# A long-convolution block and a token MLP on one core: the shift filter as diagonal matrices on TensorE, and spectra with real and imaginary parts on the partition halves

## The chip, the cores and the metric

The kernel runs on one core of a Trainium2 chip. The metric is the device time of one execution in microseconds (us). The kernel before was timed in three runs; where one number stands for it, it is their median.

## The reference, cut to what matters

All activations are bf16, S = 2048 rows by D = 448 channels.

```
q' = layernorm(x)                                 # x = A_q
k_shift[t] = sum over j=0..3 of k[t-j] * shift_k[:, j]     # causal, 4 taps per channel
kv = k_shift * v
y  = irfft(rfft(pad(kv)) * rfft(pad(ssm_k)))[:S]  # per channel, length 2S
y  = y + kv * ssm_D
h  = x + q' * y
u  = gelu(layernorm(layernorm(h)) mixed over tokens with w1 (2048x1792) + b1)
out = h + (u mixed with w2 (1792x2048) + b2)
```

So there are two parts: a convolution along the sequence by a spectrum product, and an MLP that mixes tokens. The parameter A_ssm_D is added into the filter at its first tap.

## The kernel before, in words

**Layout.** A row t of the sequence is q*16 + r, with q on the 128 partitions and r = 0..15 as a free dimension. All data lie in one SBUF tensor called arena, cut by byte offsets, so every instruction of the profile shows arena and ps (PSUM, eight banks of 448 f32 used).

**Fourier transform in two stages.** Stage 1 (emit_stage1) multiplies each r by two 128x128 tables E (cosine and sine over q), 2 matmuls of 448 columns, L933. It is done for the filter ssm_k (tag k, 16 values of r) and for kv (tag u, 16). A PSUM pair of 896 f32 is evacuated by ScalarE alone (L943) into one of eight ring buffers, and DMA transfers scatter it over partitions (L947): one of 112 rows from the POOL queue, and one of 16 rows from SP's. When all r of a tag have landed, stage 2 (emit_stage2, L964) combines them with the table FW. Its matmuls are tiled by columns: FW's left half makes real parts and its right half imaginary parts, each for 64 partitions, and two j share the partitions (par). So the real and imaginary part of a frequency lie on the same partition. The results go back over their inputs TK (filter) and TU (u), by evac, on ScalarE or VectorE (L652 to L656).

**The filter's transposes.** emit_kT transposes ssm_k, loaded as KN, on TensorE (L914) into eight PSUM banks, each for two values of r; a bank is complete when all four channel blocks have come.

**The shift filter (emit_kv).** k is loaded with a halo of three rows as KH (19 rows per partition). The four tap rows are spread to all partitions by four matmuls with a row of ones (L868). For each r VectorE multiplies four shifted rows by the taps, 1792 elements (L879); TensorE adds the four by matmuls with the identity (L885); VectorE multiplies the sum from PSUM by v, in place in V (L888). V is stage 1's input for u.

**Spectrum product and first inverse stage (emit_products_i1).** VectorE forms all four products of real and imaginary parts, 1792 elements (L1015). Matmuls tiled by rows, 64 partitions each (L1027), combine them with the tables MA, MN and MB. The results are evacuated to TU and scattered to TZ by DMA (L1051; the last pair of j in smaller transfers per half of channels, L1040, from three queues). emit_ct makes the transposed tables ET for the last stage. Before the last stage TensorE runs 34 filler matmuls (emit_warm, L1061) while the transfers land.

**Last stage and MLP.** emit_i2 (L1118) makes y for each r, then gate, residual and norms give Q. emit_mlp runs 112 + 112 matmuls with the halves W1A and W1B of w1 (L1218, L1228) and gelu (L1208), and 224 with w2 (L1238), with the residual by VectorE (L1242). w1 and w2 are loaded by SP (emit_w1_load, emit_w2_load): the first half of W1A after the last POOL transfer of u's stage 1, the rest after the last POOL transfer of i1.

**What sets the order.** All operations are recorded first, with what they read and write. A list scheduler then runs a model with estimated durations and writes a fixed order for every engine. Priorities are due times, the constants T_..., smaller first: T_K1 and T_DK1 for the filter's stage 1, T_U1 for u's, T_U2 and T_K2 for the two stage 2, T_I1 for products, T_KV for the shift filter. Operations recorded with FX = ("act", "dve") may go to either engine. In hardware each engine keeps that order and waits on semaphores. SP's queue carries all loads and the small shuffle transfers; POOL carries the large shuffle transfers and small arithmetic.

Of the kernel before, what the change touches and what calls it, by code (L numbers as in the profile page):

```python
# [509 lines left out]
def _build(nc, A_q, A_k, A_v, A_shift_k, A_ssm_k, A_ssm_D, B_w1, B_b1, B_w2, B_b2, out):  # L510
# [8 lines left out]
    R = 16  # L519
# [18 lines left out]
    o_W1A = 0  # L538
# [4 lines left out]
    o_W1B = o_V  # L543
    o_E = o_V + 14336
    o_WT = o_E + 8192
    o_SK = o_WT + 3584
# [14 lines left out]
    o_SM = o_BD + 4 * 256  # L561
# [4 lines left out]
    with ctx:  # L566
# [20 lines left out]
        KH = view(o_KH, [R + 3, D])  # L587
# [4 lines left out]
        TK = view(o_TK, [R, 2, D])  # L592
        W1B = view(o_W1B, [R, 896])
# [8 lines left out]
        WT = view(o_WT, [4, D])  # L602
        SK = view(o_SK, [4 * D])
# [4 lines left out]
        FW, MA, MB, MN = [view(o_BD + 256 * k, [128], f16) for k in range(4)]  # L608
# [30 lines left out]
        T_KV, T_DKV, T_KT, T_K1, T_DK1, T_U1, T_DU1 = -37.75, 0.96, -26.42, -39.56, 0.44, 2.72, 0.9  # L639
        T_K2, T_U2, T_D2, T_CT, T_BIAS, T_I1, T_DI1 = 29.29, -14.6, 1.375, 22.37, 56.3, 7.01, 0.974  # L640
        T_Q, T_DQ, T_I2, T_DI2, T_M1, T_W1 = 83.98, 14.35, 85.76, 0.401, 102.98, 122.45

        T_TH, T_TN = -36.0, -30.0
# [17 lines left out]
        def emit_tables():  # L661
# [125 lines left out]
            for k, (dst, i) in enumerate(((FW, 0), (MA, 1), (MB, 1))):  # L787
# [3 lines left out]
            op("pool", lambda e, W: e.tensor_scalar(out=MN, in0=MA, scalar1=-1.0, scalar2=None, op0=ALU.mult),  # L791
               r=[(o_BD + 256, 256)], w=[(o_BD + 768, 256)], n=128)
# [6 lines left out]
        r_iv = [(o_BD + 256, 768)]  # L799
# [4 lines left out]
        def emit_loads():  # L804
            Dq = "sp"
            for i, c in enumerate((3, 0, 1, 2)):
# [4 lines left out]
            op(Dq, lambda e, W: e.dma_start(SK[0:1, :], A_shift_k.rearrange("(a d) j -> a (d j)", a=1)),  # L811
               w=[(o_SK, 3584)], dmab=3584, keng=1)
            op("pool", lambda e, W: e.memset(KH[0:1, 0:3, :], 0.0), w=[(o_KH, 3 * DB, "halo")], n=3 * D)
            for c in range(4):
                sch.t0 = -14.0 + c
                op(Dq, lambda e, W, c=c: e.dma_start(KH[:, 3 + 4 * c:7 + 4 * c, :], k2d[:, 4 * c:4 * c + 4, :]),
                   w=[(o_KH + (3 + 4 * c) * DB, 4 * DB)], dmab=128 * 4 * DB)
                if c == 3:
                    sch.t0 = -10.5
                    op(Dq, lambda e, W: e.dma_start(KH[1:113, 0:3, :], k2d[0:112, 13:16, :]),  # L820
# [14 lines left out]
        def emit_xload():  # L835
            for c in range(4):
                sch.t0 = T_XL + c
                op("sp", lambda e, W, c=c: e.dma_start(X[:, 4 * c:4 * c + 4, :], x2d[:, 4 * c:4 * c + 4, :]),
                   w=[(o_X + 4 * c * DB, 4 * DB)], dmab=128 * 4 * DB,
                   after=[shuf["upool15"]])  # L840

        o_b1n = small(256)
        o_b2n = small(32)
        o_b2c = small(64)
        o_b1c = small(64)
# [452 lines left out]
```

## Time and profile before

| what | us |
|---|---|
| median of three runs | 191.09 (188.78, 191.09, 193.0) |
| span of the profiled execution, first to last instruction | 186.8 |
| busy PE / DVE / ACT / POOL | 173.8 / 109.9 / 97.3 / 72.0 |
| first stage-1 evacuation (L943) starts | 15.6 |
| first L964 (filter stage 2) starts | 39.7 |
| last product with v (L888) starts | 46.5 |
| last stage-1 transfer issued from POOL | 50.4 |
| last L1015 ends | 80.0 |
| i2 (L1118) starts | 87.8 |
| last L1242 ends | 184.6 |

The page does not give a time of the profiled execution beside its span; the median of the runs is 4.3 us above the span. In the profile PE is TensorE's matmuls, PEld its weight loads, DVE VectorE, ACT ScalarE, POOL GpSimd, SP the engine that issues most transfers. A group's row gives line, engine, operation, output and input, count, busy time, mean duration of one, and idle time ahead of it with what ended it. Matmuls overlap, so 352 ns for one is not its cost: 224 of them take 42.39 us in the chain of work that ended last. Most of evac's work stands under L652 and L653 (ScalarE) and L655 and L656 (VectorE), whichever stage it serves.

### The profile page before, as it was taken

What the parts mean: (1) busy time and instruction counts of PE and PEld (TensorE: products, weight loads), DVE (VectorE), ACT (ScalarE), POOL (GpSimd) and SP (SyncE); (2) the same over time, 40 slices, a digit from 0 to 9 for tenths busy, and PEclk for the clock granted to TensorE, in tenths of its full rate; (3) what the DMA queues carried; (4) which work ended last, traced back from release to release, by engine and by line L of the source; (5) the groups of instructions that cost most, each with busy time, mean ns of one, the idle gap of its engine ahead of it and who ended that gap; (6) DMA issues with size and microseconds to landing.
All of it is one profiled execution on the core that took longest, in us unless ns stands there. A gap on an engine that the chain in (4) does not pass through costs nothing.

```text
span 186.8 us, 2835 instructions
## 1 busy us (share of the span) xinstructions
PE 173.8 (93%) x1033; PEld 91.8 (49%) x1033; DVE 109.9 (59%) x181; ACT 97.3 (52%) x141; POOL 72.0 (39%) x177
## 2 busy tenths in 40 slices
PE   7998897998988989899989999999999999999993
PEld 2753342343332433244435445555557777777772
DVE  8877999787789999997979756000001122212221
ACT  3597989988889989950886483442121000000000
POOL 8946976699520044587178676000000000000000
DMA  5998698888549916773999999900000100111111
GB/s 140 419 418 303 179 244 219 228 226 250 141 111 383 365 49 194 220 233 102 329 400 401 423 421 422 364 4 0 0 0 4 49 32 17 49 53 49 49 49 49
DMA packets 15893, 35.44 MB, mean 190 GB/s; under 512 B 3901, under 2 KB 10062, under 8 KB 15878
## 3 DMA queue, kind: packets, MB, share of 16 engines
q1 hardware_dynamic: 11222, 25.66, 36.5%
q0 software_dynamic: 4608, 9.56, 18.3%
q8 instruction: 8, 0.13, 0.3%
q14 instruction: 7, 0.06, 0.1%
q10 hardware_dynamic: 48, 0.03, 0.0%
HBM read 22.37 MB, written 1.84 MB: 130 GB/s over the span
## 4 chain that ended last, share of the span: by engine, by line
PE 72%; DMA 9%; ACT 7%; DVE 6%; POOL 2%; issue 2%; SPq 0%; ACTq 0%
PE ps L1238 23%; PE ps L1228 11%; PE ps L1218 10%; DMA arena<-arena 7%; PE ps L1061 5%; PE ps L1027 5%; ACT arena L652 4%; PE ps L964 4%; PE ps L1118 3%; PE ps L914 2%; DMA arena<-in_A_ssm_k_dram 2%; PE ps L885 2%; DVE arena L1015 2%; POOL arena L947 2%; PE ps L933 2%
## 5 line engine op out<-in xcount | busy, mean ns | idle before, releaser
L1242 DVE SCALAR_TENSOR_TENSOR arena<-ps,arena 128x448 bf16<-128x448 f32 x16 | 10.9, 683 | 56.9 <-PE ps L1238 56.9
L1238 PE MATMUL ps<-arena 128*128 128x448 bf16 x224 | 42.5, 352 | 0.0
L1238 PEld LDWEIGHTS ps<-arena 128*128 128x128 bf16 x224 | 32.3, 144 | 10.1
L943 ACT CAST arena<-ps 128x896 bf16<-128x896 f32 x32 | 26.8, 927 | 3.6 <-PE ps L933 1.7
L652 ACT CAST arena<-ps 128x896 bf16<-128x896 f32 (+1 forms) x26 | 22.0, 908 | 2.6 <-PE ps L868 1.7
L1218 PE MATMUL ps<-arena 128*128 128x448 bf16 x112 | 23.0, 353 | 0.3 <-DVE arena L1173 0.2
L947 POOL DMA_DIRECT2D arena<-arena x32 | 19.2, 601 | 7.6 <-ACT arena L943 4.9
L1228 PE MATMUL ps<-arena 128*128 128x448 bf16 x112 | 21.4, 352 | 0.0
L1208 ACT ACTIVATE arena<-ps,arena 128x448 bf16<-128x448 f32 x14 | 8.2, 640 | 20.1 <-PE ps L1228 14.7
L879 DVE TENSOR_TENSOR arena<-arena 128x1792 bf16<-128x1792 bf16 x16 | 18.2, 1175 | 0.0
L964 PE MATMUL ps<-arena 128*64 128x448 bf16 x128 | 16.4, 361 | 1.8 <-ACT arena L652 1.0
L1125 ACT ACTIVATE arena<-ps,arena 128x448 f32<-128x448 f32 x16 | 11.2, 723 | 12.2 <-PE ps L1118 9.2
L933 PE MATMUL ps<-arena 128*128 128x448 bf16 x64 | 16.1, 355 | 1.3 <-ACT arena L943 1.3
L885 PE MATMUL ps<-arena 128*128 128x448 bf16 x64 | 14.5, 353 | 2.4 <-ACT arena L943 1.8
L1015 DVE TENSOR_TENSOR arena<-arena 128x1792 bf16<-128x1792 bf16 x16 | 16.4, 1083 | 0.0
L1218 PEld LDWEIGHTS ps<-arena 128*128 128x128 bf16 x112 | 10.9, 98 | 11.1 <-DVE arena L1173 1.1
L1051 POOL DMA_DIRECT2D arena<-arena x14 | 8.2, 588 | 20.8 <-PE ps L964 15.6
L1228 PEld LDWEIGHTS ps<-arena 128*128 128x128 bf16 x112 | 11.0, 98 | 10.2
L1027 PE MATMUL ps<-arena 64*128 64x448 bf16 x128 | 14.1, 351 | 1.3 <-DVE arena L1015 0.6
L1132 DVE SCALAR_TENSOR_TENSOR arena<-arena 128x448 f32<-128x448 bf16 x16 | 10.7, 676 | 4.7 <-ACT arena L1125 4.7
L655 DVE CAST arena<-ps 128x896 bf16<-128x896 f32 (+2 forms) x11 | 9.5, 875 | 2.7 <-PE ps L868 1.2
L964 PEld LDWEIGHTS ps<-arena 128*64 128x64 f16 x128 | 5.4, 108 | 11.4 <-ACT arena L652 4.6
(88 smaller groups left out, 200.7 us busy)
## 6 DMA issues: line engine op xcount, KB each, us to landing
arena<-arena POOLq DMA_DIRECT2D x46, 196.0 KB, 5.1
arena<-in_B_w_dram SPq DMA_DIRECT2D x8, 896.0 KB, 9.2
arena<-in_B_w_dram SPq DMA_DIRECT2D x2, 2048.0 KB, 17.2
arena<-in_B_w_dram SPq DMA_DIRECT2D x2, 1536.0 KB, 19.9
arena<-in_A_k_dram SPq DMA_DIRECT2D x4, 448.0 KB, 7.5
arena<-in_A_v_dram SPq DMA_DIRECT2D x4, 448.0 KB, 8.1
arena<-in_A_q_dram SPq DMA_DIRECT2D x4, 448.0 KB, 4.9
out_dram<-arena SPq DMA_DIRECT2D x7, 224.0 KB, 1.9
```

The costliest lines, as they stand in the source:

```text
L652: return e.copy(out=dst(), in_=src())
L879: op("dve", lambda e, W, T=T, i=i, r=r: e.tensor_tensor(out=T[:, i], in0=KH[:, r:r + 4, :], in1=WT, op=ALU.mult), r=[(o_KH + r * DB, 4 * D ...
L885: op("pe", lambda e, W, b=b, T=T, i=i, j=j: e.matmul(Pb(b, i), ID, T[:, i, j, :], start=(j == 0), stop=(j == 3)), r=[(o_ID, 256), (o + (i ...
L933: op("pe", lambda e, W, b=b, r=r, h=h, dl=dl: e.matmul(Pb(b, h), E[:, 2 * r + h, :], src[:, r, :], start=True, stop=not dl), r=[r_E(r), (o ...
L943: return e.copy(out=dst, in_=Ppair(b)) if W == "act" else e.tensor_copy(out=dst, in_=Ppair(b))
L947: shuf[tag + q_ + str(r)] = shuf[tag + q_] = op(q_, lambda e, W, w=w, p0=p0, a=a, b_=b_, j0=j0: e.dma_start(T[p0:p0 + 29:4, j0:j0 + (b_ - ...
L964: op("pe", lambda e, W, b=bs[h], h=h, j=j, c=c, par=par: e.matmul(PS[64 * par:64 * par + 64, b.slots[c], 0:D], FW[:, 64 * c:64 * c + 64], ...
L1015: op("dve", lambda e, W, m=m, i=i: e.tensor_tensor(out=MR(m.slots[0]).rearrange("p (x y) d -> p x y d", x=2), in0=TU[:, i].unsqueeze(2).br ...
L1027: k = op("pe", lambda e, W, b=bs[h], m=ms[h], par=par, t=t, tab=tab, xy=xy, P=P: e.matmul(Pb(b, par), tab[P, :], MR(m.slots[0])[P, xy, :], ...
L1218: op("pe", lambda e, W, r=r, fc=fc, b=bs[fc]: e.matmul(Pb(b), W1A[:, r, 128 * fc:128 * fc + 128], Q[:, r, :], start=(r == 0), stop=(r == R ...
L1228: op("pe", lambda e, W, r=r, fc=fc, b=b: e.matmul(Pb(b), W1B[:, r, 128 * (fc - n0):128 * (fc - n0) + 128], Q[:, r, :], start=(r == 0), sto ...
L1238: op("pe", lambda e, W, r=r, fc=fc, b=b: e.matmul(Pb(b), W2[fc // 7][:, fc % 7, r:S:R], G[:, fc, :], start=(fc == 0), stop=(fc == NFC - 1) ...
```

## The change

Three things are changed together, and due times with them.

1. **Shift filter.** k is loaded without halo. It is transposed on TensorE, 64 transposes of 128 rows by 112 channels, and evacuated to KX with channels on the partitions; a column of zeros stands where row −1 would be. A table DG holds for each block of 112 channels four diagonal matrices of taps. Matmuls of KX against DG, seven for each group of four r and block of channels, add all taps of all shifts in PSUM, with rows on the partitions again. VectorE multiplies by v as before.
2. **Spectra.** Stage 2 uses FW whole: one PSUM pair for each j, real parts on partitions 0–63 and imaginary parts on 64–127. The product needs the filter also with the halves exchanged: KS, filled from TK by eight transfers on SP's queue, two for each four j (N_SW). One product of 1792 elements makes both sums' terms, and four full matmuls for each j replace the tiled ones. Half of MA changes sign, and MN falls away.
3. **Others.** Stage 1's evacuation may go to either engine. The filter's transposes are evacuated by blocks of eight r and one channel block. The last transfers of i1 are like the others. W1A and W1B change places in the arena, since KS lies at its beginning.

The diff, cut to its core:

```diff
-    o_W1A = 0
+    o_KS = 0
+    o_W1B = 0
...
-    o_W1B = o_V
+    o_W1A = o_V
...
-        T_KV, T_DKV, T_KT, T_K1, T_DK1, T_U1, T_DU1 = -37.75, 0.96, -26.42, -39.56, 0.44, 2.72, 0.9
-        T_K2, T_U2, T_D2, T_CT, T_BIAS, T_I1, T_DI1 = 29.29, -14.6, 1.375, 22.37, 56.3, 7.01, 0.974
-        T_Q, T_DQ, T_I2, T_DI2, T_M1, T_W1 = 83.98, 14.35, 85.76, 0.401, 102.98, 122.45
-        T_TH, T_TN = -36.0, -30.0
+        T_KV, T_DKV, T_KT, T_K1, T_DK1, T_U1, T_DU1 = -35.67, 2.8, -45.99, -40.62, 0.9, -24, 0.433
+        T_K2, T_U2, T_D2, T_CT, T_BIAS, T_I1, T_DI1 = 45.17, -14.6, 1.375, 8.48, 50.16, 8.91, 1.558
+        T_Q, T_DQ, T_I2, T_DI2, T_M1, T_W1 = 80.1, 14.35, 82.13, 0.501, 102.98, 122.45
+        T_TH, T_TN = -45.27, -29.29
+        N_SW = 4
+        T_KX = -39.65
...
-            op("pool", lambda e, W: e.tensor_scalar(out=MN, in0=MA, scalar1=-1.0, scalar2=None, op0=ALU.mult),
+            op("dve", lambda e, W: e.tensor_scalar(out=MA[64:128], in0=MA[64:128], scalar1=-1.0, scalar2=None, op0=ALU.mult),
...
+            op("dve", lambda e, W: e.tensor_tensor(
+                out=DG[0:112].rearrange("p c j d -> p (c j) d"), in0=ID[0:112, 0:112].unsqueeze(1).broadcast_to([112, 16, 112]),
+                in1=wsc[0:112].unsqueeze(2).broadcast_to([112, 16, 112]), op=ALU.mult),
+               r=[(o_ID, 256), (o_wsc, 64)], w=[(o_DG, 3584)], n=1792, kind="1x")
+            for g in (3, 0, 1, 2):
+                for cc in range(2):
...
+                            op("pe", lambda e, W, b=b, i=i, rr=rr, r=r, c=c: e.transpose(
+                                out=Pbf(b, 0)[0:112, 512 * i + 128 * rr:512 * i + 128 * rr + 128],
+                                in_=KH[:, r, 112 * c:112 * c + 112], identity=ID),
...
+            for g in range(4):
+                for cc in range(2):
...
+                        for dl in (0, -3, -2, -1, 1, 2, 3):
...
+                            op("pe", lambda e, W, b=b, i=i, cc=cc, dl=dl, i0=i0, i1=i1, rs=rs, sh=sh: e.matmul(
+                                Pb(b, i)[:, 112 * i0:112 * i1 + 112], KX[cc][0:112, i, rs, sh:sh + 128],
+                                DG[0:112, 2 * cc + i, i0 - dl:i1 - dl + 1, :].rearrange("p j d -> p (j d)"),
+                                start=(dl == 0), stop=(dl == 3)),
...
-                op("act", fn, br=[b], bw=[w], n=2 * D, kind="psum")
+                op(FX, fn, br=[b], bw=[w], n=2 * D, kind="psum")
...
+            for j in range(R):
+                sch.t0 = (T_K2 if scale else T_U2) + T_D2 * j
+                b = _Buf(psum, 2)
                 for h in range(2):
+                    op("pe", lambda e, W, b=b, h=h, j=j: e.matmul(Pb(b, h), FW, T[:, j, h, :], start=True, stop=True),
+                       r=r_fw + [(o_T + (2 * j + h) * DB, DB)], bw=[b], n=D)
+                evac(lambda j=j: T[:, j], lambda b=b: Ppair(b), [(o_T + j * 2 * DB, 2 * DB)], b, 2 * D, scale=scale)
+                if scale and j % N_SW == N_SW - 1:
+                    j0 = j + 1 - N_SW
+                    for h in range(2):
+                        op("sp", lambda e, W, j0=j0, h=h: e.dma_start(
+                            KS[64 * h:64 * h + 64, j0:j0 + N_SW].rearrange("p j c d -> p (j c d)"),
+                            TK[64 - 64 * h:128 - 64 * h, j0:j0 + N_SW].rearrange("p j c d -> p (j c d)")),
...
+                op("dve", lambda e, W, m=m, j=j: e.tensor_tensor(
+                    out=MR(m.slots[0]).rearrange("p (x h) d -> p x (h d)", x=2),
+                    in0=TU[:, j].rearrange("p h d -> p (h d)").unsqueeze(1).broadcast_to([128, 2, 2 * D]),
+                    in1=KK[:, :, j * 2 * D:(j + 1) * 2 * D], op=ALU.mult),
...
+                for x, tab in enumerate((MB, MA)):
                     for h in range(2):
+                        k = op("pe", lambda e, W, b=b, m=m, h=h, x=x, tab=tab: e.matmul(
+                            Pb(b, h), tab, MR(m.slots[0])[:, 2 * x + h, :], start=(x == 0), stop=(x == 1)),
+                           r=r_iv, br=[m], bw=[b], n=D)
```

## The prediction

> **What bounds the kernel now.** I read the page first (busy shares, the forty slices), then the chain that ended last in order of time, then the busy time of each engine by stretch, then the groups with shapes kept apart. The page's forty slices part the span into a front and an MLP:
>
> ```profile
> PE   7998897998988989899989999999999999999993
> DVE  8877999787789999997979756000001122212221
> ACT  3597989988889989950886483442121000000000
> DMA  5998698888549916773999999900000100111111
> ```
>
> From slice 20 on TensorE is full and the rest is nearly idle. That part is 448 matmuls at 0.19 us (chain: L1218, L1228 and L1238; 42.39 us for 224 of them), and the change does not touch it. So only the start of i2, the inverse stage, counts. It stands at 87.78 us and the end follows 99.0 us later. I cut the front at the marks that the timeline gives: first stage-1 evacuation (15.6), first stage-2 result of u (54.0), last i1 evacuation (82.0), first i2 matmul (87.8). The columns are length, then busy us (instructions) of PE, PEld, DVE, ACT, POOL, granted clock, DMA share, GB/s:
>
> ```profile
> 15.60:54.00 38.40, 33.84 (x192) 13.77 (x190) 32.93 (x36) 34.72 (x43) 29.18 (x56) 1.00 0.74 210
> 54.00:82.00 28.00, 25.27 (x221) 9.64 (x222) 26.46 (x31) 26.32 (x31) 8.72 (x15) 1.00 0.71 231
> 82.00:87.80 5.80, 5.73 (x32) 2.79 (x30) 5.35 (x17) 0.00 (x0) 5.55 (x13) 1.00 0.52 160
> ```
>
> In both long stretches VectorE and ScalarE are the fullest (DVE 86% and 94%, ACT 90% and 94%). PE's busy time counts overlapping 352 ns matmuls; at the chain's 0.19 us each its work in the first stretch is about 30 us of 38.4. The third stretch is one latency: the last results' way through the DMA, covered on PE by 34 fillers of L1061. The chain shows how u reaches its end:
>
> ```profile
> 41.55 0.77 PE ps L885 x4
> 42.31 0.02 issue
> 42.34 1.09 DVE arena L888
> 43.43 2.01 DVE arena L879
> 45.44 0.04 issue
> 45.48 0.93 PE ps L885 x4
> ...
> 47.85 0.50 PE ps L933 x2
> 48.35 0.02 issue
> 48.38 0.92 ACT arena L943
> ```
>
> The shift filter's products (L879) stand on VectorE ahead of the last u matmuls (L933). The groups concerned, with count, busy us, mean ns, idle before:
>
> ```profile
> L879 DVE TENSOR_TENSOR arena<-arena 128x1792 bf16<-128x1792 bf16 x16 | 18.2, 1175 | 0.0
> L943 ACT CAST arena<-ps 128x896 bf16<-128x896 f32 x32 | 26.8, 927 | 3.6 <-PE ps L933 1.7 <-PE ps L937 1.4 <-DMA arena<-arena 0.4
> L888 DVE TENSOR_TENSOR arena<-ps,arena 128x896 bf16<-128x896 f32 x8 | 8.7, 1090 | 3.1 <-PE ps L885 3.0
> L1015 DVE TENSOR_TENSOR arena<-arena 128x1792 bf16<-128x1792 bf16 x16 | 16.4, 1083 | 0.0
> L655 DVE COPY arena<-ps 128x1024 f16<-128x1024 f16 x1 | 0.7, 678 | 0.0
> L652 ACT COPY arena<-ps 128x1024 f16<-128x1024 f16 x3 | 3.0, 1012 | 1.4 <-PE ps L996 1.4
> ```
>
> L879 never waits: VectorE is always late there.
>
> [...] L879 and L1015 take 1.08 to 1.18 us for 1792 elements, L888 1.09 us for 896. [...] 448 KB loads land after 4.9 us (q) and 7.5 us (k). [...] No 64-partition transfer is in the trace before.
>
> **The change, part by part.**
>
> *Removed from VectorE:* 16 L879, 18.2 us, one of them before 15.6; so 17 us from the first stretch. Four tap-row evacuations (L655 three at 0.62, L652 one at 0.53) leave the time before 15.6. *Added:* eight evacuations of transposed k, 1024 elements bf16 from PSUM: 1.01 us on ACT, 0.68 on DVE (the last two rows above), 0.85 as a mean, 6.8 us. One product that makes the diagonals, 1792 elements with an f32 factor: L751 has 1024 elements of 32 bits in 1.21 us, so 1.2 to 2.1 us; I take 2.0, half of it before 15.6. The sign flip of half a table moves from POOL (0.58) to DVE, between 0.15 us (L742, one element) and 0.28 (L783, 128 elements); 0.2. The eight L888 and all other evacuations keep number and size; those of transposed ssm_k become six of 1024 and two of 512 in place of eight of 896, the same sum. Net on the two engines from 15.6: −17 + 6.8 + 1.0 + 0.2 = −9.0 us. L943 may now also go to DVE, so the saving can be shared. The two engines carry 120.4 us in the 66.4 us from 15.6 to 82.0, a density of 0.907 each. At equal density, (120.4 − 9.0)/(2 × 0.907) = 61.4 us: **−5.0 us**. If the saving stays on DVE while ACT's 61.0 us remain, it is near 0; if the density rises too, −7. I keep −5.0.
>
> *TensorE.* Off: four L868 at 0.48 us, 1.9 us, all in the chain. The filter's 64 matmuls of 448 columns become 112 with the same 28,672 columns; at 0.19 us per 448 that is 12.1 us[...]; I take 13, +0.9. 64 transposes at 0.062 us (chain: 0.74 us for 12 L914): +4.0. Stage 2: 128 tiled matmuls at 0.124 (0.99 us for 8) become 64 at 0.19, −3.7 in two stages. i1: 128 at 0.105 (4.20 us for 40) become 64 at 0.19, −1.2. Sum about −1.9 us, but +3 in the first stretch, where PE has about 8 us left; it is hidden behind the evacuations, else costs those 3.
>
> *The start.* Without the 1.9 us of L868 and without the halo loads (294 and 39 KB, landing 10.8 us after issue), but with the diagonals ahead of u and fresh PSUM evacuations per half: between −2 and +1; **−1.2 us**.
>
> *The exchanged copy.* Eight SP issues of 458,752 B each, 3.67 MB. A pair of halves: [...]7.5 us by the k-load row. Each waits for four evacuations of the filter's stage 2, and behind it in SP's order stand the small parts of u's shuffles, whose landing u2 awaits, then the x and w1 loads. The product L1015 gains a wait: behind it on DVE are evacuations, and i1's matmuls wait for it. In bytes it takes 8.7 us of all DMA engines at 420 GB/s (the load slices), 13 at 282 (210 GB/s over a share of 0.74). The DMA has 26% of 38.4 = 10 us free in stretch one and 8 in stretch two. So it fits mostly in the gaps; it gives nothing back, since it only adds bytes and a wait, and at most it is the 4.8 to 7.4 us of rival (b). I take **+1.2 us**.
>
> *The tail.* The last pair's transfers are no longer cut in half-width pieces: they land after the normal median 5.1 us, not 4.5: **+0.6**, between 0 and 1.5. The two or three issues it saves on POOL and ACT are hidden by L1061.
>
> *Moved at no cost:* both halves of w1 change place. The first is loaded over V, last read at 49.1 and loaded at 55.7; the second over the copy, last read at 80.0 and loaded at 89.1. Covered by these gaps; uncovered, a w1 quarter costs its 9.2 us landing. POOL loses a 1.2 us memset and a table and gains small ones; its 32 shuffle issues every 0.81 us (0.59 and a 0.22 gap) need 26 us of stretch one, so POOL is next in line when that stretch falls under about 30. ACT's finer share needs no waits beyond PSUM.
>
> **Sum:** −5.0 − 1.2 + 1.2 + 0.6 = −4.4 us. The profile's span is 186.8; the profiled execution's whole time is not given, and the runs' median lies 4.3 us above the span, which I take as what lies around it: 191.1. With −4.4 it is **186.7 us**.
>
> **The rivals.**
> (a) *The DMA, or PE, takes over stretch one.* 28.4 us of DMA there (0.74 × 38.4) plus 8.7 to 13 for the copy is 37 to 41 us: if all of the copy falls before u2, u's shuffles end no sooner, and only the gain on stretch two is left. For it: 0.78 share already in 30 to 50 us. Against it: slices 10 and 11 are at 5 and 4 tenths. Time 190.0.
> (b) *The copy of the last filter group comes late: slower.* In the profile the last four filter evacuations (L653) run from 68.7 to 76.1, after u2, since filter stage 2 has the lowest priority; it keeps it. If so again, landing adds 4.9 to 7.5 us (81 to 83.6); then four products at 1.03, four matmuls and an evacuation (5.8 us): 86.8 to 89.4 in place of 82.0. With little gained ahead of it: 196 to 198.5, say 197. It decides if that group is evacuated after about 70 us. Against it: VectorE, relieved, has room before u2.
> (c) *More is freed than summed.* All of filter stage 2 goes before u2, so stretch two holds 32 evacuations and 16 products: 22.4 us at full density against 28, and stretch one still shrinks by three: 182.
> That the work does not leave VectorE is excluded: L879 is gone from the code.
>
> **Numbers.** Forecast 0.43 (range of its own 183 to 189.5), (a) 0.19, (b) 0.30, (c) 0.08. A difference of 2%, about what a measurement of this kernel can tell from no change, is 187.3 below and 194.9 above. Of the forecast's 0.43, 0.30 lie below 187.3; with (c), faster 0.38. Same: 0.13 + 0.19 = 0.32. Slower 0.30. The range 183 to 197 leaves out about half of (c) and half of (b), 0.19.
>
> **What would show it.** Right: no DVE group of sixteen 1.1 us products ahead of u; casts of stage 1 on both engines; u2 starting at 50 to 52 and i2 at about 83.4; MLP still 99.0 us long. The start: first stage-1 evacuation by 14.5. Wrong by (a): u2 at 54 or later with a DMA share above 0.9 in stretch one. Wrong by (b): DVE or PE idle before L1015's successor, ended by a DMA arena<-arena, and the filter's last evacuation after 70. Wrong by the tail: more than 6.5 us from the last i1 evacuation to i2.

## The result, and the profile after

The changed kernel took 202.51 us (median of four runs, 200.81 to 205.7), the kernel before beside it 190.7. The ratio is **1.068, interval 1.057 to 1.080**: slower by 6.8%, where 186.7 us and faster were forecast. Executions of one kernel differ (31 of the kernel before took 188.05 to 193.23 us), so ratios, here and below, compare only those within about 1.5% of a kernel's fastest; the medians of all runs give 1.062 here. The profiled execution of the changed kernel was the longest of its four (205.7 us, span 203.9), so a few of the microseconds in its trace are its own; the runs without a profile had spans from 199.0 to 201.2.

The page's forty slices of the kernel after (5.1 us each), with the granted TensorE clock in tenths:

```profile
PE   7998997994998895007998899999999999999994
DVE  8897967664789993009939787610000122222221
PEclk9999999999599999755999999999999999999999
DMA  5996667696799999980559999980000011111111
```

Before, PE was full from slice 20 on; now there is a hole in PE and DVE in slices 15 to 17 (counted from 0) in which the DMA is full, and two dips of the clock, in slice 10 and in 16 to 18. The same cuts as before, at the marks of this kernel (first stage-1 evacuation 14.5, first evacuation of u2 57.4, last i1 matmul 98.6, i2 105.2); columns: length, busy us (instructions) of PE, PEld, DVE, ACT, POOL, granted clock, DMA share, GB/s:

```profile
14.50:57.36 42.86, 37.75 (x266) 21.36 (x265) 29.80 (x38) 30.15 (x36) 26.54 (x53) 0.92 0.74 213
57.36:98.58 41.22, 25.38 (x103) 8.58 (x101) 27.30 (x34) 24.18 (x28) 8.26 (x14) 0.83 0.88 231
98.58:105.23 6.65, 6.61 (x35) 3.44 (x36) 4.72 (x14) 0.93 (x2) 5.80 (x12) 1.00 0.46 124
```

Stretch one is 42.9 us where it was 38.4, although VectorE and ScalarE are now busy for 70% of it and no longer 86 and 90%: the work that the forecast took away is gone, and the time isn't. Stretch two is 41.2 us where it was 28.0, with the DMA at 0.88 and every engine half idle. From i2 to the end are 98.7 us, as before. So the whole difference lies ahead of i2, which starts at 105.2 in place of 87.8. The groups with shapes kept apart:

```profile
L1031 DVE TENSOR_TENSOR arena<-arena 128x1792 bf16<-128x1792 bf16 x16 | 16.3, 1083 | 13.6 <-DMA arena<-arena 13.6
L964 ACT CAST arena<-ps 128x896 bf16<-128x896 f32 x20 | 17.3, 908 | 9.6 <-PE ps L954 6.0 <-DMA arena<-arena 2.4 <-PE ps L902 1.1
L964 DVE CAST arena<-ps 128x896 bf16<-128x896 f32 x12 | 13.0, 1087 | 6.5 <-PE ps L954 3.0 <-PE ps L1017 1.8 <-PE ps L858 1.6
L908 DVE TENSOR_TENSOR arena<-ps,arena 128x896 bf16<-128x896 f32 x8 | 8.7, 1092 | 4.6 <-PE ps L902 4.3
```

The product (L1031, before L1015) now waits 13.6 us for a transfer, and it is one wait. Stage 1's evacuations (L964, before L943) go to both engines, and both wait for TensorE there. The chain that ended last, in order of time, shows where the product's wait lies:

```profile
51.13 6.77 PE ps L982 x20
...
69.65 0.49 SPq L988
70.14 0.04 issue
70.19 21.60 DMA arena<-arena
...
91.87 1.10 DVE arena L1031
92.97 0.04 issue
93.02 5.56 PE ps L1042 x16
98.58 0.05 issue
98.62 6.61 PE ps L1059 x34
```

The last of the eight exchanging copies (L988) is issued at 70.2 and lands 21.6 us later; four products, their matmuls and the fillers follow. Twenty stage-2 matmuls take 6.77 us and sixteen of i1 5.56: 0.34 and 0.35 us each, where those of the MLP take 0.19. The granted clock over these two pieces is 0.58 and 0.57; from 106 to 190 us, in the last stage and the MLP, it is 1.00. What SP's queue held around the copies (start, length, what, count):

```profile
52.70 4.67 SPq L988 DMA_DIRECT2D arena<-arena  x4
57.41 3.63 SPq L838 DMA_DIRECT2D arena<-in_A_q_dram  x4
61.14 1.11 SPq L988 DMA_DIRECT2D arena<-arena  x2
62.28 1.14 SPq L1190 DMA_DIRECT2D arena<-in_B_w_dram  x2
68.02 0.75 SPq L1049 DMA_DIRECT2D arena<-arena  x1
69.65 1.13 SPq L988 DMA_DIRECT2D arena<-arena  x2
```

Ahead of the last two copies went four loads of x (L838) and the first two loads of W1A (L1190), 3.7 MB together by their sizes of 448 and 896 KB.

### The profile page after: what moved, and what is told of

Same layout as the page of the kernel before. It is cut to its first block, busy times and chain, and to the rows that moved or that the text cites. A ratio compares the mean times of both kernels' runs of the same rounds, so it can differ in the third digit from the quotient of the medians.

```text
span 203.9 us, 2772 instructions
## 1 busy us (share of the span) xinstructions
PE 177.1 (87%) x1013; PEld 99.8 (49%) x1013; DVE 106.9 (52%) x178; ACT 92.8 (46%) x134; POOL 69.5 (34%) x176
## 4 chain that ended last, share of the span: by engine, by line
PE 61%; DMA 21%; DVE 5%; ACT 4%; SPq 3%; issue 2%; POOL 2%; ACTq 0%; DVEq 0%
PE ps L1236 21%; DMA arena<-arena 16%; PE ps L1226 10%; PE ps L1216 10%; DMA arena<-in_A_k_dram 5%; PE ps L1059 5%; PE ps L982 4%; PE ps L1116 3%; PE ps L1042 3%; PE ps L902 3%; ACT arena L964 2%; DVE arena L661 2%; DVE arena L908 1%; DVE arena L1031 1%; PE ps L954 1%
## 5 line engine op out<-in xcount | busy, mean ns | idle before, releaser
L1236 PE MATMUL ps<-arena 128*128 128x448 bf16 x224 | 42.5, 352 | 0.0
L1240 DVE SCALAR_TENSOR_TENSOR arena<-ps,arena 128x448 bf16<-128x448 f32 x16 | 10.9, 684 | 56.1 <-PE ps L1236 56.1
L1236 PEld LDWEIGHTS ps<-arena 128*128 128x128 bf16 x224 | 32.3, 144 | 10.1
L1042 PE MATMUL ps<-arena 128*128 128x448 bf16 x64 | 16.7, 399 | 15.0 <-DVE arena L1031 14.3
L1031 DVE TENSOR_TENSOR arena<-arena 128x1792 bf16<-128x1792 bf16 x16 | 16.3, 1083 | 13.6 <-DMA arena<-arena 13.6
L1216 PE MATMUL ps<-arena 128*128 128x448 bf16 x112 | 23.0, 352 | 0.0
L968 POOL DMA_DIRECT2D arena<-arena x32 | 19.3, 605 | 10.7 <-ACT arena L964 5.6
L1049 POOL DMA_DIRECT2D arena<-arena x16 | 9.5, 593 | 38.7 <-ACT arena L658 38.1
L964 ACT CAST arena<-ps 128x896 bf16<-128x896 f32 x20 | 17.3, 908 | 9.6 <-PE ps L954 6.0
L1226 PE MATMUL ps<-arena 128*128 128x448 bf16 x112 | 21.5, 352 | 0.0
L982 PE MATMUL ps<-arena 128*128 128x448 bf16 x64 | 16.9, 409 | 3.0 <-DVE arena L964 2.1
L1042 PEld LDWEIGHTS ps<-arena 128*128 128x128 f16 x64 | 5.9, 108 | 25.8 <-DVE arena L1031 20.5
L1206 ACT ACTIVATE arena<-ps,arena 128x448 bf16<-128x448 f32 x14 | 8.2, 640 | 19.4 <-PE ps L1226 14.5
L964 DVE CAST arena<-ps 128x896 bf16<-128x896 f32 x12 | 13.0, 1087 | 6.5 <-PE ps L954 3.0
L954 PE MATMUL ps<-arena 128*128 128x448 bf16 x64 | 15.2, 354 | 1.5 <-ACT arena L964 1.2
L1216 PEld LDWEIGHTS ps<-arena 128*128 128x128 bf16 x112 | 10.9, 98 | 10.4 <-DVE arena L1171 0.3
L902 PE MATMUL ps<-arena 112*128 112x224 bf16 (+3 forms) x112 | 13.9, 273 | 0.1
L982 PEld LDWEIGHTS ps<-arena 128*128 128x128 f16 x64 | 5.8, 108 | 12.9 <-issue 3.1
```

The lines of the kernel that those rows point to most:

```text
L902: op("pe", lambda e, W, b=b, i=i, cc=cc, dl=dl, i0=i0, i1=i1, rs=rs, sh=sh: e.matmul(Pb(b, i)[:, 112 * i0:112 * i1 + 112], KX[cc][0:112, i ...
L954: op("pe", lambda e, W, b=b, r=r, h=h, dl=dl: e.matmul(Pb(b, h), E[:, 2 * r + h, :], src[:, r, :], start=True, stop=not dl), r=[r_E(r), (o ...
L964: return e.copy(out=dst, in_=Ppair(b)) if W == "act" else e.tensor_copy(out=dst, in_=Ppair(b))
L968: shuf[tag + q_ + str(r)] = shuf[tag + q_] = op(q_, lambda e, W, w=w, p0=p0, a=a, b_=b_, j0=j0: e.dma_start(T[p0:p0 + 29:4, j0:j0 + (b_ - ...
L982: op("pe", lambda e, W, b=b, h=h, j=j: e.matmul(Pb(b, h), FW, T[:, j, h, :], start=True, stop=True), r=r_fw + [(o_T + (2 * j + h) * DB, DB ...
L1031: op("dve", lambda e, W, m=m, j=j: e.tensor_tensor(out=MR(m.slots[0]).rearrange("p (x h) d -> p x (h d)", x=2), in0=TU[:, j].rearrange("p ...
```

## The experiments

Two questions had to be parted: what the exchange costs and why, and why stretch one didn't shorten. "Earlier" and "later" are told by the start of i2 and by the first product, since the 99 us after i2 stay. A caution holds for all of them: the planner writes the order anew for every kernel, and the due times were not searched anew. Where two traces have the same order of work on the engines, the text says so.

### What the exchange costs

**Without the exchange.** The copies are left out, and the product reads TK in both places. The terms that need the exchanged halves are not computed.

```diff
-                    for h in range(2):
-                        op("sp", lambda e, W, j0=j0, h=h: e.dma_start(
-                            KS[64 * h:64 * h + 64, j0:j0 + N_SW].rearrange("p j c d -> p (j c d)"),
...
-                    in1=KK[:, :, j * 2 * D:(j + 1) * 2 * D], op=ALU.mult),
+                    in1=TK[:, j].rearrange("p h d -> p (h d)").unsqueeze(1).broadcast_to([128, 2, 2 * D]), op=ALU.mult),
```

> The changed kernel with the eight exchange transfers left out; the product multiplies TK twice, so the exchanged halves are not computed. Theory A (the last exchange transfers come late, and VectorE and TensorE stand for them): the 13.6 us wait ahead of L1031 and the half clock behind it vanish, i2 starts at about 84 to 88 us instead of 105, and the time falls from 202.5 to 183-189. Rival B (the loss is in the earlier stretch, stage 1 and shift filter, and the transfer is only where it shows): i2 starts no earlier than 95, time 194 or more.

Measured: 191.3 us, ratio 1.009 (1.005 to 1.013); i2 starts at 90.1, between the ranges of the two theories. Ahead of i2 PE, DVE, ACT and POOL do the same work in the same order as in the changed kernel. The product's row:

```profile
L1023 DVE TENSOR_TENSOR arena<-arena 128x1792 bf16<-128x1792 bf16 x16 | 16.2, 1084 | 0.0
```

The wait is gone. So 11 of the change's 13 us (0.060 of the ratio's 0.068, times 190) belong to the exchange. And the other half of the forecast fell here too: without the exchange all the rest of the change, counted at −5.6 us, gave +1.7.

**Each half of the change alone.** filter_only is the kernel before with part 1 and the first two points of part 3; spectra_only is the kernel before with part 2 and the last two points. Each keeps the rest as before; spectra_only has the due times of before too, filter_only those of the changed kernel but for the line with T_K2 and T_I1. The core of filter_only against the kernel before:

```diff
-                    op("dve", lambda e, W, T=T, i=i, r=r: e.tensor_tensor(out=T[:, i], in0=KH[:, r:r + 4, :], in1=WT,
+                        for dl in (0, -3, -2, -1, 1, 2, 3):
...
-                op("act", fn, br=[b], bw=[w], n=2 * D, kind="psum")
+                op(FX, fn, br=[b], bw=[w], n=2 * D, kind="psum")
```

And of spectra_only:

```diff
-                            for par in range(2):
+                    op("pe", lambda e, W, b=b, h=h, j=j: e.matmul(Pb(b, h), FW, T[:, j, h, :], start=True, stop=True),
...
+                if scale and j % N_SW == N_SW - 1:
+                    j0 = j + 1 - N_SW
```

> The kernel before with only the new shift filter (transposes, diagonals, stage-1 evacuation on either engine, evacuation of the filter's transposes by channel block), and the spectra, product and last transfers of before. If the shift filter is a gain that the exchange hides: 184-188. If taking 17 us from VectorE gave nothing because the POOL issues, transfers or TensorE set that stretch: 189-193. If the new filter is itself slower: above 194.

> The kernel before with only the spectra on partition halves and the exchange by DMA; shift filter of before on VectorE. Theory A (the exchange is all of the loss): at or above the changed kernel, 200-207. Rival (loss in the shift filter's part): 190-195.

Measured: filter_only 194.77 us, ratio 1.027 (1.019 to 1.035), i2 at 93.5. spectra_only 210.11 us, ratio 1.110 (1.097 to 1.123), i2 at 107.9. Each half alone makes the kernel slower. The chain of spectra_only has the late copy twice:

```profile
63.02 15.79 DMA arena<-arena
78.81 0.02 issue
78.83 1.10 DVE arena L1014
...
85.10 0.50 SPq L971
85.60 0.04 issue
85.64 9.54 DMA arena<-arena
```

Here the filter's stage 2 has the due time of before, and its last group is evacuated at 84 us: rival (b) of the prediction in its plain form.

**The filter's stage 2 earlier.** Only its due time is changed, so that its groups, and with them the copies, come ahead of u2.

```diff
-        T_K2, T_U2, T_D2, T_CT, T_BIAS, T_I1, T_DI1 = 45.17, -14.6, 1.375, 8.48, 50.16, 8.91, 1.558
+        T_K2, T_U2, T_D2, T_CT, T_BIAS, T_I1, T_DI1 = -16.0, -14.6, 1.375, 8.48, 50.16, 8.91, 1.558
```

> The changed kernel with one constant altered: due time T_K2 from 45.17 to -16.0, so that the filter's stage 2 goes level with u's and its last exchange transfers are issued before the x and w1 loads and before the shuffles of i1. Theory A: last exchange lands before about 75 us, no long wait of L1031, time 188-194. Rival B' (the bytes of the exchange themselves are the price, wherever they stand): they delay other transfers instead, and the time stays above 197.

Measured: median 199.12 us. The four runs took 194.2, 197.6, 200.6 and 202.8 us, at granted clocks of 0.998, 0.983, 0.974 and 0.966; the profiled one is the longest (i2 at 100.0). The 16 products now run from 69.5 to 88.2 with no wait for a copy (0.2 us for PE). In this trace others wait instead, as rival B' had it: in the chain two pieces of 10.34 and 6.85 us of DMA stand between i1 and i2, and i1's transfers (L1049) land after, min/median/max:

```profile
DMA to landing us min/median/max: 6.6/8.8/10.5
```

They take 3.0/4.6/6.0 us in nocopy. How much the exchange costs in time here can't be read from runs that differ so.

**W1A later.** In the changed kernel the first two loads of W1A are put behind the last transfer of i1.

```diff
-                       after=[shuf["upool15" if h < 2 else "zpool"]])
+                       after=[shuf["zpool"]])
```

> The changed kernel with the first half of W1A loaded behind the last transfer of i1, like the second, so that 1.84 MB leave SP's queue ahead of the last two exchange transfers. If the place in the queue makes them late: their landing, 21.6 us after issue, falls by 4.4 us (1.84 MB at 420 GB/s) or more, the wait of L1031 from 13.6 to 9 or less, time 196-199. If the half rate of the exchange and i1's shuffles alone make them late: landing stays above 19 us, time 201-204.

Measured: 197.82 us, ratio 1.040 (1.034 to 1.046); i2 at 93.3, 11.9 us sooner than in the profiled changed kernel, which was the longest of its runs; by the ratios 2.8% are won, some 5 us. PE, DVE, ACT and POOL keep their order ahead of i2. The landing of the eight copies, min/median/max:

```profile
DMA to landing us min/median/max: 4.8/7.5/10.7
```

It was 5.5/9.4/21.6, with nearly the same times of issue (54.3 to 70.8). So the 1.8 MB of loads issued ahead of them in SP's queue made the last copies late, and not their own issue. The 10.9 us between the two are more than the 4.4 that the expectation put for these bytes; whether the rest comes from the order in the queue or from that one execution isn't shown. What was won isn't all kept: the span, 195.0, is 2.7 us longer than i2's start and 99.0, since the MLP then waits for W1A.

**Half of the exchange on another queue.** In early_k2 the copies to partitions 64–127 go to POOL's queue.

```diff
-                        op("sp", lambda e, W, j0=j0, h=h: e.dma_start(
+                        op(("sp", "pool")[h], lambda e, W, j0=j0, h=h: e.dma_start(
```

> The kernel early_k2 with the second half of each exchange issued from POOL's queue instead of SP's, so that both directions between the partition halves run at once. Theory E ([...]the 7168-byte packets of the exchange took 533 ns, 13.4 bytes per ns and engine, where 3584-byte packets took 140 ns, 25.6 bytes per ns): mixed directions bring the packets to about 300 ns, and the time from 199 to 193-196. Rival (SBUF-to-SBUF packets of this size are slow by themselves, or POOL's issues cost as much): packets stay near 500 ns, time 198-202.

Measured: 193.91 us, ratio 1.018 (1.013 to 1.024), i2 at 92.8. The time lies in theory E's range, but the quickest run of early_k2 took 194.2, so a gain by the second queue isn't shown. The reason fails: the packets took 454 ns and not 300, as the next table shows, and with the same two queues in the last run below (two_k1first) 538. Against nocopy's 1.009 this kernel leaves about 1% for the whole exchange, where the changed kernel pays 6.0%: most of that cost lay in when the copies ran and what they met.

**The same bytes straight across.** In early_k2 each two copies of 64 partitions become one copy of 128 partitions; the exchanged halves are not computed.

```diff
-                            KS[64 * h:64 * h + 64, j0:j0 + N_SW].rearrange("p j c d -> p (j c d)"),
-                            TK[64 - 64 * h:128 - 64 * h, j0:j0 + N_SW].rearrange("p j c d -> p (j c d)")),
+                            KS[:, j0:j0 + N_SW].rearrange("p j c d -> p (j c d)"),
+                            TK[:, j0:j0 + N_SW].rearrange("p j c d -> p (j c d)")),
```

> early_k2 with each pair of exchanging copies (two of 64 partitions, upper half to lower and back) replaced by one copy of all 128 partitions straight across, of the same 512 packets of 7168 bytes; the product then takes unexchanged halves as its second operand, so the halves it needs are not computed. Theory P (a copy whose two sides lie on 64 partitions each is what makes a packet slow): a packet falls from 533 ns to 270 to 320 (the 24 to 26 bytes per ns of the other packets), the sum of the packets from 16 to 8 or 10 us of all engines, and i2 starts 4 us or more before the 100.0 of early_k2. Rival S (a long packet between two places in SBUF costs this much whatever its partitions): a packet stays at 450 to 540 ns, and i2 starts at 98 or later.

Measured: one run, 193.01 us, i2 at 91.8. It is 1.2 us under the quickest run of early_k2, so a gain in time isn't shown; what the run shows is the packets. PE, DVE, ACT and POOL have the order of early_k2. The copies of straight, then of early_k2:

```profile
L988 SPq DMA_DIRECT2D arena<-arena x4: 465/494/549, 53.6 to 60.5; - x4
DMA to landing us min/median/max: 4.6/5.0/5.5
```

```profile
L988 SPq DMA_DIRECT2D arena<-arena x8: 467/1332/1830, 57.7 to 71.9; - x8
DMA to landing us min/median/max: 5.5/7.8/12.1
```

Twice the bytes per copy land in 5.0 us and not in 7.8. From the records of single DMA packets in the traces, the 512 packets of 7168 bytes that make up the exchange, and for comparison the packets of 3584 bytes (most of them loads of k, v and x):

```
kernel         median ns of a packet   sum over 16 engines, us
after                 513                    16.4
spectra_only          522                    16.8
w1_late               514                    16.3
early_k2              533                    16.0
two_queues            454                    15.0
two_k1first           538                    17.0
straight              274                     9.5
3584-byte packets, all of these: 140 ns (25.6 bytes per ns)
```

Theory P holds: a packet of the same size, between the same two tiles, takes 274 ns (26 bytes per ns) where the copy spans all partitions, and 513 to 533 (13 to 14 bytes per ns) where each side of it lies on 64. The long packet by itself is not slow. Nor is it the crossing, which straight leaves out too: the shuffle's transfers from POOL's queue cross partitions, and their packets of 5376 bytes take 215 ns (25 bytes per ns, median) in the changed kernel. The other transfers feel it: i1's (L1049) now land after

```profile
DMA to landing us min/median/max: 3.7/4.8/5.6
```

where early_k2 had 6.6/8.8/10.5. Why a packet between the halves takes about twice as long, 513 to 533 ns against 274, the runs do not show.

### Why stretch one did not shorten

**The ring filled earlier.** In filter_only both engines' stage-1 evacuations waited 10.0 us for ring buffers (DMA arena<-arena, 4 times). The filter's stage 1 gets due times closer together.

```diff
-        T_KV, T_DKV, T_KT, T_K1, T_DK1, T_U1, T_DU1 = -35.67, 2.8, -45.99, -40.62, 0.9, -24, 0.433
+        T_KV, T_DKV, T_KT, T_K1, T_DK1, T_U1, T_DU1 = -35.67, 2.8, -45.99, -40.62, 0.1, -24, 0.433
```

> The kernel filter_only with one constant altered: T_DK1 from 0.9 to 0.1, so that all of the filter's stage 1 stands ahead of the shift filter's matmuls on TensorE. Theory C (in filter_only TensorE alternates 14 shift-filter matmuls, 1.70 us, with six of stage 1, 1.15 us, so stage 1's transfers come too slowly until 36 us and then all at once, and the ring of eight buffers makes both evacuating engines wait): DMA share from 20 to 35 us rises from 0.66 to 0.8 or more, the waits of stage 1's evacuation for the DMA (10.1 us) fall under 4, time 187-191. Rival D (the sum of TensorE's work in the stretch is the bound, in whatever order): 193-196.

Measured: 193.31 us, ratio 1.019 (1.012 to 1.026). The waits fell to 1.2 us, as theory C had it, and the time by 1.5, within the intervals; it lies in rival D's range. The wait for ring buffers was a symptom.

**Stage 1 on ScalarE alone**, as in the kernel before.

```diff
-                op(FX, fn, br=[b], bw=[w], n=2 * D, kind="psum")
+                op("act", fn, br=[b], bw=[w], n=2 * D, kind="psum")
```

> The kernel filter_only with stage 1's evacuation on ScalarE alone, as before. If the mixing of two engines is what stalls the transfers (POOL and SP issue in a fixed order and wait for the slower engine, 4.8 us on DVE in filter_only): 189-192. If the saving on VectorE is then not shared and ScalarE is the bound: 195-199. Theory C says that it changes little: 193-197.

Measured: 193.93 us, ratio 1.021 (1.016 to 1.025). Sharing the evacuations between the engines or not is worth less than can be told apart here, so it isn't what holds the stretch with the new filter.

**Half the shuffled bytes**, in the kernel before and in filter_k1first.

```diff
-                        T[p0:p0 + 29:4, j0:j0 + (b_ - a) // 8].rearrange("p j c d -> p j (c d)"),
-                        WR(w.slots[0])[a:b_].rearrange("p c d -> p (c d)")),
+                        T[p0:p0 + 29:4, j0:j0 + (b_ - a) // 8, 0, :],
+                        WR(w.slots[0])[a:b_, 0, :]),
```

> The kernel before, but stage one's transfers carry only the first half of each row (896 of 1792 bytes a packet) and stage two reads that half twice; half of the shuffled data is left out. Theory D (stretch one of the kernel before is bound by the evacuations on VectorE, as the prediction had it): the last POOL issue of the shuffle stays within 2 us of 50.4 and the time within 2 us of the kernel before. Rival T (it is bound by the transfers already): the last issue comes at 46 or sooner and the time falls by 4 us or more.

> filter_k1first (only the shift filter is new) with the same halved transfers as before_half; half of the shuffled data is left out. Theory T' (with VectorE relieved the transfers bound stretch one, so the 5 us that the prediction counted were not to be had): the first u2 comes at 50 or sooner against 55.2, and the time is 3.5 us or more under filter_k1first's 193.3. Rival O (TensorE, its added work and its lower clock bound it): u2 stays at 53.5 or later and the time within 1.5 us of 193.3.

Measured: before_half 188.7 us, ratio 0.9995 (0.996 to 1.003); filter_half 192.88 us, ratio 1.020 (1.014 to 1.025). All engines keep their order in both pairs. Neither kernel is bound by these transfers alone; theory T' fell, and so did rival T for the kernel before. Nor was the clock low, as rival O had it: from 13 to 56 us it was 1.00 in filter_k1first and in filter_half (0.54 from 50 to 55 us in filter_only). Before_half's chain shows how level the stretch was already: the chain of the kernel before has one long piece of transfers,

```profile
20.95 13.37 DMA arena<-arena x2
```

and in before_half none is left in that time; pieces of TensorE and ScalarE fill it, and i2 starts at 87.9 in place of 87.8.

**Fewer filter matmuls**, with all bytes and with half of them: two of the seven matmuls for each piece are kept.

```diff
-                        for dl in (0, -3, -2, -1, 1, 2, 3):
+                        for dl in (0, 3):
```

> filter_k1first with two of the seven diagonal matmuls for each piece of the shift filter (the unshifted one and the one shifted by three rows, 32 matmuls in place of 112); the other taps are left out. VectorE, ScalarE and the transfers keep their work. Theory P (with the new filter TensorE bounds stretch one: its 13.6 us of filter matmuls, transposes and stage one leave it some 5 us free of 43): TensorE loses some 9 us there, the first product comes at 55.5 or sooner against 58.8, and the time is 190.3 or less against 193.3. Rival T (transfers and TensorE both bound it): within 1.5 us of 193.3, and only filter_fewtaps_half falls. Rival E (neither: the order of the evacuations): both stay within 1.5 us.

> filter_half with the same two of seven filter matmuls; half of the shuffled data and the other taps are left out. Theory P: as filter_fewtaps, within 1.5 us of it, since the transfers do not bind. Rival T: 3 us or more under both filter_half's 192.9 and filter_fewtaps. Rival E: within 1.5 us of 192.9.

Measured: filter_fewtaps 193.52 us, ratio 1.013 (1.008 to 1.018), its first product at 60.5; filter_fewtaps_half 189.7 us, ratio **0.999 (0.994 to 1.003)**, first product at 56.1. Theory P (TensorE alone) fell, and the times are those of rival T: either relief alone brings 0.6% at most, within the intervals; both together 2.0% against filter_k1first. The order tells how far this reaches. It is the same in filter_k1first and filter_half, where half the bytes bring nothing, and the same in filter_fewtaps and filter_fewtaps_half, where they bring 1.5%; but fewer matmuls made the planner write another order from 28 us on, so what TensorE's relief does by itself was not seen. The chains agree with rival T. With the bytes halved TensorE stands for most of filter_half's chain from 24.6 to 47.1 us (19.2 of 22.5), first of all in

```profile
25.96 7.64 PE ps L899 x70
```

and with the matmuls cut the transfers stand in filter_fewtaps's for 16.7 us:

```profile
21.82 4.75 DMA arena<-arena
...
27.06 8.24 DMA arena<-arena
...
38.04 3.66 DMA arena<-arena
```

So with the new filter TensorE and the transfers are level in stretch one, each hiding the other; a share of the planner's order isn't ruled out. Busy times from 13 to 56 us (columns as above) of before, filter_k1first and filter_half:

```profile
13.00:56.00 43.00, 38.39 (x234) 16.21 (x233) 36.70 (x45) 37.88 (x47) 29.69 (x57) 1.00 0.74 216
```

```profile
13.00:56.00 43.00, 38.30 (x306) 21.44 (x306) 30.66 (x40) 31.84 (x39) 28.16 (x58) 1.00 0.72 210
```

```profile
13.00:56.00 43.00, 38.38 (x307) 21.45 (x307) 32.11 (x42) 31.55 (x39) 27.92 (x55) 1.00 0.46 144
```

PE's column doesn't move: 38.3 of 43 us with the new filter too, while DVE and ACT fall by 6 us each in the second kernel and the DMA's share by a third in the last. It counts overlapping matmuls (in the changed kernel 352 ns for one of L1236, and 42.5 us busy for its 224) and was as high before, so it shows little by itself; the chains weigh more.

**VectorE relieved in the kernel before.** One tap is multiplied in place of four; TensorE adds it four times, so its count stays. The other taps are left out.

```diff
-                    op("dve", lambda e, W, T=T, i=i, r=r: e.tensor_tensor(out=T[:, i], in0=KH[:, r:r + 4, :], in1=WT,
+                    op("dve", lambda e, W, T=T, i=i, r=r: e.tensor_tensor(out=T[:, i, 0, :], in0=KH[:, r, :], in1=WT[:, 0, :],
...
-                        op("pe", lambda e, W, b=b, T=T, i=i, j=j: e.matmul(Pb(b, i), ID, T[:, i, j, :], start=(j == 0),
+                        op("pe", lambda e, W, b=b, T=T, i=i, j=j: e.matmul(Pb(b, i), ID, T[:, i, 0, :], start=(j == 0),
```

> The kernel before with one tap of its shift filter multiplied on VectorE in place of four (448 elements in place of 1792, some 13.7 us less VectorE work); TensorE adds that one product four times, as many matmuls as before, and the other taps are left out. Theory D (VectorE and ScalarE bound stretch one, as the prediction had it): at equal density 13.7 us of two engines' work are 7.5 us; of these at least 3 show, and the time is 186.5 or less. Rival O (TensorE or the order of the work bounds the stretch as soon as VectorE is relieved): the time stays within 1.5 us of the kernel before, so that relieving VectorE bought nothing even without added matmuls.

Measured: 195.47 us, ratio 1.030 (1.021 to 1.039): **slower**, which neither theory had. The products with v and stage 1's evacuations of this kernel (min/median/max ns, first and last start):

```profile
L888 DVE TENSOR_TENSOR arena<-ps,arena x8: 1087/1092/1094, 21.8 to 35.6; 128x896 bf16<-128x896 f32 x8
```

```profile
L943 ACT CAST arena<-ps x32: 887/924/1036, 15.9 to 49.5; 128x896 bf16<-128x896 f32 x32
```

In the kernel before the last L888 starts at 46.5 and the last L943 at 49.2. So v's product was done 11 us sooner and stage 1 was not done any sooner. From 30 to 50 us VectorE is busy for 6.4 us (16.9 before), and the chain runs elsewhere:

```profile
41.26 0.59 POOL arena L947
41.85 0.32 POOL arena L985
42.17 6.51 DMA arena<-arena
```

The planner, told of a shorter operation, wrote another order: TensorE ran 24 of the filter's matmuls in one piece (L885, 4.71 us in the chain, from 30.9), the transfers of u came in a row, one POOL issue each 0.81 us, and an evacuation waited for the ring. Why the new order is worse by 5 us than the old one was only argued from this. Shown is that this relief of VectorE, with the order that it led to, did not shorten the stretch; with the order of before held fixed it was not tried.

**The best of the parts together:** two_queues with filter_k1first's due times.

```diff
-        T_KV, T_DKV, T_KT, T_K1, T_DK1, T_U1, T_DU1 = -35.67, 2.8, -45.99, -40.62, 0.9, -24, 0.433
+        T_KV, T_DKV, T_KT, T_K1, T_DK1, T_U1, T_DU1 = -35.67, 2.8, -45.99, -40.62, 0.1, -24, 0.433
```

> two_queues with the schedule of stage one of filter_k1first (due-time step of the filter's transform 0.1 in place of 0.9), so that the ring fills early. If the two gains add, as they should where they lie in different stretches (filter_k1first gained 1.5 us on filter_only before u2, two_queues gained on the exchange after it), the time is 192 to 193 and the ratio to the kernel before 1.005 to 1.012. If the earlier shuffle only moves the wait to the exchange, as it would if transfers bound both stretches, the time stays at 193.5 to 195. Neither theory has it under 190.

Measured: 195.29 us, ratio 1.030 (1.021 to 1.038), above both theories' ranges. The gains don't add; this is rather worse than two_queues (1.018). No complete version of the change was found that is as fast as the kernel before.

## Why the prediction was wrong, by its steps

The forecast missed by 15.8 us by the medians, by 17 by the ratio. By nocopy, about 7 of these lie in "−5.0" and what stood around it (−5.6 counted for all but the copy, +1.7 measured), and about 10 in the exchanged copy (+1.2 counted, 11 measured).

**"At equal density" failed.** The work did leave the engines: VectorE and ScalarE carried 74.6 us from 13 to 56 before and 62.5 in filter_k1first. What failed is the division by 0.907. It took the fullest engines for the bound and let the stretch shrink until they were as full again. Their density fell to 0.73 in place of that. The path spoke against it: in the chain of the kernel before, VectorE stands for 5.2 of the 38.4 us of stretch one, and L879 for 2.0 of them; the lines that the prediction read begin behind the 13.37 us of transfers. The prediction's own sentence, near 0 if the saving stays on VectorE, was nearer; before_onetap, in another order, even shows a loss with 12 us of VectorE's filter work gone (18.2 to 6.1). Columns of 86 and 90% beside others at 88 (PE) and 0.74 (DMA) marked several uses that are nearly level here, joined by buffers and a fixed order, and not one bound.

**"It is hidden behind the evacuations, else costs those 3" failed in its first half.** The sizes were right: 14 filter matmuls take 1.69 to 1.72 us, 13.6 for 112 (13 forecast), and the groups L964 and L908 then wait for TensorE. This is rival (a), whose place was right; its 190.0 was low by some 3 us against filter_k1first. Of its signs one came, u2 after 54 (57.4), and one didn't: the DMA share stayed at 0.74 and did not pass 0.9. It named one of DMA or PE; by the runs both are level there.

**The copy: "fits mostly in the gaps" failed, twice.** Its load was taken from 282 to 420 GB/s of the other transfers, 8.7 to 13 us of all engines; with packets of 513 ns it is 16.4. So the time that it takes from everybody else's transfers was mis-sized by a factor of 1.3 to 1.9. Then its landing: 7.5 us forecast by the row of the k loads, 9.4 the median, 21.6 the last. This is **rival (b)**, in its place (DVE waits for a DMA ahead of the last products) and its sign, with a last group evacuated at 69.6, right at the "about 70" that was to decide. Its price was too small, because "behind it in SP's order stand … the x and w1 loads" was seen from the wrong side: for the last copies these loads stand ahead. w1_late shows it. The forecast had left (b) a chance of 0.30, and 197 us.

**"Moved at no cost" failed for W1A.** In the kernel before its first half went as early, at 55.7, but with no copy behind it. Now its bytes cost the last copies 10.9 us of landing in the profiled runs (21.6 to 10.7); put late, it costs the MLP 2.7 us.

**Right:** the start (first evacuation 14.5, −1.1 us; −1.2 forecast); the evacuations of transposed k (0.68 us on DVE, 1.02 on ACT); the MLP's length (98.7). The product for the diagonals took 2.39 us for 2.0. The tail's +0.6 was not seen: from the end of the last i1 evacuation (99.5) to i2 are 5.7 us, 5.8 before. Not in the sum at all: the clock. Twenty stage-2 and sixteen i1 matmuls at 0.34 and 0.35 us in place of 0.19, at a granted 0.58 and 0.57, are some 3.0 and 2.5 us in the profiled execution.

## What to carry to other kernels

When a stage's engines stand at 86, 88 and 90% with the DMA at three quarters, don't divide what is saved by a density: ask for each of the others what it would need alone, look who stands in the chain, and count on nothing from relieving one of them until a run shows it. Price a new transfer twice, by its landing and by the time that it takes from the other transfers, and look at what goes ahead of the last one of them in its queue: here the last copy landed after 21.6 us with 1.8 MB of loads ahead of it, and after at most 10.7 without. A packet of a copy between two halves of the partitions took 513 to 533 ns here, and 274 straight across; a layout that needs such a copy has to save more than it costs.

## What the runs showed of the hardware that was not expected

- Copies of 64 partitions to the other 64: 13 to 14 bytes per ns and engine (7168 bytes in 513 to 533 ns; 454 and 538 in two kernels with two queues), against 26 straight across all 128 (274 ns).
- The same copy, issued at nearly the same time (70.8 and 70.2 us), landed after at most 10.7 us or after 21.6, without and with 1.8 MB of loads ahead of it in one queue; the second figure is from an execution 1.6% longer than the median.
- In the changed kernel PE was 4 tenths busy in slice 9 and 5, 0 and 0 in slices 15 to 17; the granted clock was 5 tenths in slice 10 and 7, 5 and 5 in 16 to 18. Matmuls of 448 columns took 0.34 and 0.35 us from 51.1 and 93.0 us on, at a granted 0.58 and 0.57, and 0.19 in the MLP at 1.00. Whether the idle time is the cause was not tried by itself.
- Nearly halving the shuffle's traffic (DMA share 0.72 to 0.46, 13 to 56 us) and leaving out 80 of 112 filter matmuls each moved the time by less than 0.6%, and both together by 2.0%; the second and third with another order of work.
